# A planned attention and routing kernel: row maxima written twice, two partial sums kept in PSUM, the rests of units 0 and 1 moved to GpSimd, and the attention part written out in another order

## The chip, the cores and the metric

The kernel runs on one core of one Trainium2 chip. The metric is the time of one execution in microseconds of device time; lower is better. The engines are named as the profile names them: PE (TensorE), PEld (its weight loads), DVE (VectorE), ACT (ScalarE), POOL (GpSimd) and SP (SyncE, which here only issues DMA transfers; SPq is its queue).

## What is computed

Attention within clusters, followed by a greedy assignment of tokens to experts and an expert feed-forward layer. Cut to what matters:

```python
# q, k, v: (4, 8, 768, 64); centroids: (8, 16, 64)
q_assign = argmax(q_n @ c_n)          # cluster of each query, of each key
k_assign = argmax(k_n @ c_n)
scores = q @ k.T / 8, with -1e9 where q_assign != k_assign
scores = scores - max(scores, axis=-1)
attn = exp(scores) / (sum + 1e-9)
x = (attn @ v) as rows of 3072 tokens x 512
# experts: logits = x @ w_gate; tokens are handed out in order of
# falling logit, at most 384 per expert; then for each expert
out[mask] = relu(x[mask] @ w1[e]) @ w2[e]
```

## The kernel before

The kernel has two parts. The attention part works on eight units (a batch and four of its heads each); the part after it finds each expert's tokens, gathers their rows and runs the two matrix products. Every step of both parts is named in a long table of words, `ATT_ORDER` and `FFN_ORDER`; a loop calls the named functions one after the other, and that order is the order of the instructions on every engine. An engine takes its instructions strictly in that order; semaphores hold back an instruction whose inputs are not there.

**Splitting.** Each float32 input is scaled by 64 and split into two float16 halves, a high part and a rest: `split_hi` writes the high part on ACT (`L629`), `split_lo` the rest on DVE (`L633`, one instruction with both the loaded float32 tile and the high part as inputs). In unit 0 this is done head by head for q and k (128x384) and at once for v (128x1536); from unit 1 on each of q, k and v is one instruction of 128x1536. `load` fetches the inputs into four `ld` tiles that are used in turn, so that a load waits until the tile's former content has been split.

**Clusters and the two score products.** `cent` multiplies by the centroids, `hot0` to `hot5` (`hh` for unit 0) find the cluster of each row (`L667` to `L683`) and put a one-hot mark of +32768 or -32768 into extra columns of `qb` and `kb` (`L681`, `L683`). The four blocks qa, ka, qb, kb are transposed: by PE and copies in unit 0 (`pt`, `ptc`, `L720`, `L724` on ACT, `L726` on DVE), by DMA from unit 1 on (`trans`, `L714`). `m_mm` (`L761`) forms the scores in one layout, `m_rd` (`L765`, DVE) takes each row's maximum. `row0` and `row1` (`L775`, `L779`) turn twelve maxima into rows of a small tile `m2` (`qm` in unit 0), which `rowt` (`L783`) transposes by DMA and `row2` (`L787`) copies into rows 96 to 98 of `qbt`. `b_mm` (`L797`, `L801`) forms the scores again in the other layout, with the maxima subtracted by the matrix product, and `b_exp` (`L804`) takes the exponential on ACT. `res` (`L812`) forms the exponential's rest on POOL, and `av` (`L823` to `L829`) multiplies by v. So the second half of a unit's heads cannot begin `b_mm` before `rowt` and `row2` of that half have landed.

**Leaving a head.** `out0`, `out1`, `out2`, `hi0`, `hi1` (`L833` to `L852`) normalise a head and split it for the next product. `xtr` (`L861`) transposes two heads by DMA, `xst` (`L858`) stores them, and `lg0`, `lg1`, `lg2` (`L878`, `L885`, `L892`) add their share to the logits `L`. `lg1` sums a product from PSUM into `lt`; `lg2` adds `lt` to `L`. `vs`, `vact`, `vh2`, `vl2` (`L742` to `L752`) form a column mean of v: `vact` writes `vs`, `vh2` its high part `vmh`, `vl2` combines the two.

**Buffers that set who waits.** The score tiles `sc` have three PSUM buffers, released by `m_rd`, by `b_exp` or by a copy. The tile `mx` has one: `cent`, `vs` and `lg0` use it in turn. The accumulator `av` of a head has one, released by `hi1`. `wd` (`L652`) is a matrix product whose result nobody reads; it fills waits of PE at the start.

**The SP queue.** All loads, DMA transposes and the small transfers of the maxima stand in one queue on SP, each waiting in its place for what it needs.

Of the kernel before, what the change touches and what calls it, by code (L numbers as in the profile page):

```python
# [26 lines left out]
wd hh3,0 wd wd hh4,0,k dup,0,k,1 wd wd hh4,0,q split_lo,0,v,-,D hh5,0,k cent0,1,k hh5,0,q pt,0,kb,0 split_hi,0,q,3
pt,0,qb,0 cent0,1,q ptc,0,kb,0,A wd wd ptc,0,qb,0,D wd load,2,k,- wd split_hi,0,k,3 wd hh0,1 m_mm,0,0 dup,0,q,2 m_mm,0,1
hh1,1 m_mm,0,2 dup,0,k,2 hh2,1 wd hh3,1 wd dup,0,q,3 wd wd hh4,1,k wd hh4,1,q wd hh5,1,k split_lo,0,q,2,D vs,0 hh5,1,q
dup,0,k,3 split_lo,0,k,2,D split_lo,0,q,3,D wd wd split_lo,0,k,3,D vact,0 load,1,v,- wd wd vh2,0 wd wgs load,1,q,- wd wd  # L30
wd vl2,0 wd wd m_rd,0,0 wd wd wd wd wd m_rd,0,1 pt,0,kb,1 wd wd ptc,0,kb,1,A wd m_rd,0,2 pt,0,qb,1 wd wd ptc,0,qb,1,A wd
# [5 lines left out]
wd wd wd wd m_rd,0,3 wd wd wd wd wd m_rd,0,4 pt,0,qb,2 wd wd ptc,0,qb,2,A wd tab,9 pt,0,kb,3 tab,10 trans,1,qa,- tab,11
pt,0,qb,3 tab,12 ptc,0,kb,3,A tab,13 m_mm,0,5 ptc,0,qb,3,D wd wd dup,1,k,- m_rd,0,5 m_mm,0,6 m_mm,0,7 wd row0,0,0
m_mm,0,8 row1,0,0 m_rd,0,6 cent,1,k,0 dup,1,q,- cent,1,k,1 cent,1,k,2 m_rd,0,7 pt,0,qm,0 load,2,q,- cent,1,k,3
load,2,v,- ptc,0,qm,0,A wd m_rd,0,8 m_mm,0,9 wd split_hi,2,k,- wd wd m_rd,0,9 m_mm,0,10 m_mm,0,11 wd m_rd,0,10 m_mm,0,12  # L40
wd wd wd hot0,1,k b_mm,0,0 m_rd,0,11 wd wd b_exp,0,0 wd wd hot1,1,k m_mm,0,13 res,0,0,P wd row0,0,1 wd row1,0,1 wd
hot2,1,k wd wd m_rd,0,12 split_hi,2,q,- av,0,0 hot3,1,k pt,0,qm,1 b_mm,0,1 hot4,1,k ptc,0,qm,1,A m_rd,0,13 cent,1,q,0
hot5,1,k cent,1,q,1 cent,1,q,2 b_exp,0,1 trans,1,kb,- split_lo,2,k,-,D m_mm,0,14 cent,1,q,3 split_hi,2,v,- m_mm,0,15
b_mm,0,2 m_rd,0,14 res,0,1,P b_exp,0,2 hot0,1,q m_mm,0,16 res,0,2,P av,0,1 hot1,1,q trans,2,ka,- m_rd,0,15 av,0,2
hot2,1,q m_mm,0,17 m_rd,0,16 b_mm,0,3 dup,2,k,- hot3,1,q m_mm,0,18 hot4,1,q m_rd,0,17 load,3,q,- hot5,1,q b_exp,0,3
trans,1,qb,- row0,0,2 b_mm,0,4 row1,0,2 m_rd,0,18 res,0,3,P pt,0,qm,2 b_exp,0,4 tab,14 m_mm,0,19 tab,15 tab,16
ptc,0,qm,2,A m_mm,0,20 m_rd,0,19 res,0,4,P av,0,3 split_hi,3,k,- b_mm,0,5 m_rd,0,20 m_mm,0,21 av,0,4 m_rd,0,21 b_exp,0,5
b_mm,0,6 split_lo,2,q,-,D m_mm,0,22 b_exp,0,6 m_mm,0,23 cent,2,k,0 dup,2,q,- b_mm,0,7 m_rd,0,22 res,0,5,P cent,2,k,1
trans,2,qa,- cent,2,k,2 cent,2,k,3 b_exp,0,7 m_rd,0,23 m_mm,1,0 res,0,6,P av,0,5 row0,0,3 b_mm,0,8 row1,0,3 m_rd,1,0
pt,0,qm,3 res,0,7,P b_exp,0,8 out0,0,0 m_mm,1,1 out1,0,0 out2,0,0 ptc,0,qm,3,A b_mm,0,9 load,3,v,- m_rd,1,1 res,0,8,P  # L50
hi0,0,0 m_mm,1,2 b_exp,0,9 hi1,0,0 b_mm,0,10 m_rd,1,2 av,0,6 res,0,9,P b_exp,0,10 m_mm,1,3 tab,17 av,0,7 tab,18
split_hi,3,q,- m_rd,1,3 res,0,10,P b_mm,0,11 tab,19 tab,20 m_mm,1,4 tab,21 b_exp,0,11 hot0,2,k av,0,8 tab,22 m_rd,1,4
b_mm,0,12 tab,23 res,0,11,P m_mm,1,5 b_exp,0,12 tab,24 av,0,9 m_rd,1,5 b_mm,0,13 res,0,12,P tab,25 m_mm,1,6 b_exp,0,13
tab,26 av,0,10 m_rd,1,6 b_mm,0,14 res,0,13,P m_mm,1,7 tab,27 b_exp,0,14 av,0,11 tab,28 m_rd,1,7 b_mm,0,15 res,0,14,P
m_mm,1,8 out0,0,1 b_exp,0,15 out1,0,1 b_mm,0,16 out2,0,1 hi0,0,1 vl2,1 m_mm,1,9 split_lo,2,v,-,D b_exp,0,16 hi1,0,1
res,0,15,P load,4,k,- tab,29 xtr,0,0 av,0,12 m_rd,1,8 av,0,13 tab,30 m_rd,1,9 tab,31 b_mm,0,17 xst,0,0 res,0,16,P
m_mm,1,10 hot1,2,k b_exp,0,17 av,0,14 m_rd,1,10 b_mm,0,18 tab,32 res,0,17,P m_mm,1,11 tab,33 b_exp,0,18 av,0,15 tab,34
m_rd,1,11 b_mm,0,19 tab,35 tab,36 m_mm,1,12 row0,1,0 tab,37 b_exp,0,19 row1,1,0 av,0,16 res,0,18,P rowt,1,0 m_rd,1,12
b_mm,0,20 hot2,2,k m_mm,1,13 b_exp,0,20 av,0,17 res,0,19,P m_rd,1,13 b_mm,0,21 out0,0,2 m_mm,1,14 out1,0,2 b_exp,0,21
b_mm,0,22 res,0,20,P out2,0,2 row2,1,0 m_rd,1,14 hi0,0,2 m_mm,1,15 b_exp,0,22 res,0,21,P hi1,0,2 b_mm,0,23 m_rd,1,15  # L60
av,0,18 b_exp,0,23 av,0,19 res,0,22,P hot3,2,k m_mm,1,16 hot4,2,k av,0,20 m_rd,1,16 hot5,2,k res,0,23,P lg0,0,0 b_mm,1,0
trans,2,kb,- lg1,0,0 m_mm,1,17 b_exp,1,0 av,0,21 m_rd,1,17 b_mm,1,1 res,1,0,P cent,2,q,0 b_exp,1,1 cent,2,q,1 cent,2,q,2
cent,2,q,3 split_lo,3,k,-,D m_mm,1,18 av,0,22 b_mm,1,2 m_mm,1,19 hot0,2,q res,1,1,P trans,3,ka,- b_exp,1,2 av,0,23
hot1,2,q split_hi,3,v,- hot2,2,q res,1,2,P m_rd,1,18 dup,3,k,- hot3,2,q b_mm,1,3 hot4,2,q m_mm,1,20 load,4,q,- m_rd,1,19
hot5,2,q vs,2 b_exp,1,3 trans,2,qb,- out0,0,3 out1,0,3 out2,0,3 b_mm,1,4 res,1,3,P vact,2 m_rd,1,20 hi0,0,3 m_mm,1,21
b_exp,1,4 hi1,0,3 b_mm,1,5 vh2,2 m_rd,1,21 res,1,4,P av,1,0 b_exp,1,5 av,1,1 xtr,0,1 split_hi,4,k,- m_mm,1,22
# [1372 lines left out]
```

## Time and profile before

| what | value |
|---|---|
| median of 3 runs | 739.81 us |
| lowest and highest | 739.64 and 742.39 us |
| the profiled execution | 742.15 us |
| its span (first to last instruction) | 740.4 us |
| mean granted TensorE clock | 0.964 |
| first exponential of unit 0 | 46.0 us after the span's start |
| end of the attention part | about 437 us |

The profiled execution is 2.3 us above the median and 1.8 us above its own span. Busy time is a share of the span; a group's row gives line, engine, operation, output and inputs, count, total busy us and mean ns, and after the bar the idle time of the engine just before the group with what ended it. A row of the timeline gives start, duration and, in brackets, the idle time before it and its releaser. All positions are in us from the span's start.

### The profile page before, as it was taken

The numbers are of one execution on the slowest core, as the hardware profiler recorded it, in microseconds if no ns is written. First come the engines' busy times: TensorE is split into PE (matmuls) and PEld (weight loads), VectorE is DVE, ScalarE is ACT, GpSimd is POOL, SyncE is SP. The second block draws the span as 40 slices with busy tenths as digits, with TensorE's granted clock in tenths as the row PEclk, the third lists the DMA queues.
The fourth block names the chain that finished last, engine by engine and source line by source line (L and its number), as shares of the span: only waits on it lengthen the run. The fifth ranks groups of instructions, "written<-read, shape, count | busy, mean of one in ns | idle before, by whom it ended". The sixth has DMA issues, their size and how long they took to land. (4 is left out here: it accounts for less than half of the span.)

```text
span 740.4 us, 19763 instructions
## 1 busy us (share of the span) xinstructions
PE 669.7 (90%) x8274; PEld 444.9 (60%) x8274; DVE 545.1 (74%) x1170; ACT 420.9 (57%) x547; POOL 479.9 (65%) x369
## 2 busy tenths in 40 slices
...
GB/s 184 173 194 211 40 93 209 149 122 225 90 135 170 139 164 78 117 117 89 90 47 47 34 34 89 184 253 63 326 158 213 259 112 313 104 342 267 29 15 42
DMA packets 175451, 105.85 MB, mean 143 GB/s; under 512 B 135426, under 2 KB 160002, under 8 KB 175362
## 3 DMA queue, kind: packets, MB, share of 16 engines
...
## 5 line engine op out<-in xcount | busy, mean ns | idle before, releaser
L812 POOL TENSOR_TENSOR rt<-pt 128x768 f16<-128x768 f32 x181 | 281.4, 1571 | 139.3 <-ACT pt L804 136.4
L804 ACT ACTIVATE pt<-sc 128x768 f32<-128x768 f32 x192 | 154.6, 811 | 135.3 <-PE sc L801 120.6
L765 DVE TENSOR_REDUCE mxs<-sc 128x1 f32<-128x768 f32 x192 | 180.9, 951 | 39.5 <-PE sc L761 37.1
L823 PE MATMUL av<-vh,pt 128*128 128x66 f16 x1152 | 128.0, 196 | 9.8 <-DVE xb L852 9.8
L826 PE MATMUL av<-vh,rt 128*128 128x66 f16 x1152 | 127.7, 195 | 1.8 <-POOL rt L812 1.8
L1361 PE MATMUL pf<-xgt,w1h 128*128 128x384 f16 (+1 forms) x640 | 128.8, 293 | 0.3 <-DVE xgt L726 0.3
L825 PE MATMUL av<-vl,pt 128*128 128x64 f16 x1152 | 127.7, 194 | 0.0
L825 PEld LDWEIGHTS <-pt 128*128 128x128 bf16 x1152 | 108.1, 100 | 17.6 <-issue 8.7
L823 PEld LDWEIGHTS <-pt 128*128 128x128 bf16 x1152 | 108.8, 99 | 13.5 <-DVE xb L852 3.6
L797 PE MATMUL sc<-qbt,kbt 99*128 99x384 f16 x384 | 96.8, 334 | 17.8 <-DVE mxs L765 8.3
L826 PEld LDWEIGHTS <-rt 128*128 128x128 f16 x1152 | 107.6, 98 | 2.2 <-POOL rt L812 2.1
L761 PE MATMUL sc<-kbt,qbt 80*128 80x384 f16 x384 | 94.0, 329 | 10.2 <-DMA qbt<-qb 5.5
L801 PE MATMUL sc<-qat,kat 128*128 128x384 f16 x384 | 95.8, 331 | 0.0
L1361 PE MATMUL pf<-xgt,w1l 128*128 128x384 f16 (+1 forms) x320 | 89.9, 293 | 0.0
L1323 ACT ACTIVATE wr<-wr 128x1024 f32<-128x1024 f32 x64 | 66.7, 1046 | 24.9 <-PE pc L1279 23.2
L1361 PEld LDWEIGHTS <-w1h 128*128 128x128 f16 x640 | 57.3, 97 | 28.7 <-issue 1.1
L1399 PE MATMUL pf<-w2h,hh 128*128 128x512 f16 x192 | 72.6, 378 | 0.0
L1399 PE MATMUL pf<-w2l,hh 128*128 128x512 f16 x192 | 72.5, 378 | 0.0
L1399 PE MATMUL pf<-w2h,hl 128*128 128x512 f16 x192 | 72.5, 378 | 0.0
L1333 POOL TENSOR_TENSOR w2l<-wr,w2h 128x1024 f16<-128x1024 f32 x32 | 67.7, 2136 | 1.8 <-ACT w2h L1326 1.5
L1333 POOL TENSOR_TENSOR w1l<-wr,w1h 128x1024 f16<-128x1024 f32 x32 | 67.6, 2139 | 0.2
L1337 POOL DMA_INDIRECT xg<-xrow,idx x24 | 23.3, 972 | 60.6 <-DVE idx L1296 22.4
...
## 6 DMA issues: line engine op xcount, KB each, us to landing
...
xg<-xrow,idx POOLq DMA_INDIRECT x24, 6.3
```

Source lines behind the costliest of these rows:

```text
L761: nc.tensor.matmul(p[:, half, :S // 2], QBT[u][:D + C, i, :], KBT[u][:D + C, h * J + half * 3:h * J + half * 3 + 3, :], start=True, stop=True)
L765: nc.vector.tensor_reduce(mxs[u % 3][:, i:i + 1], MP.pop((u, i))[:, :, :S // 2], axis=AX.XY, op=OP.max)
L797: nc.tensor.matmul(ps[:, half, :S // 2], KBT[u][:ER + 3, s, :], QBT[u][:ER + 3, cs, :], start=True, stop=False)
L801: nc.tensor.matmul(ps[:, half, :S // 2], KAT[u][:, s, :], QAT[u][:, cs, :], start=False, stop=True)
L804: nc.scalar.activation(pts[(u * 12 + s // 2) % RP][:, s % 2], MP.pop((u, "b", s))[:, :, :S // 2], AF.Exp, scale=ESC)
L812: (nc.vector if e == "D" else nc.gpsimd).tensor_sub(rts[x][:, s % 2], p.rearrange("p a b -> p (a b)"), hi_view(pts[x])[:, s % 2])
L823: nc.tensor.matmul(o[:, j, :], hi[:, js], VH[u][:, s, :], start=(kt == 0 and j == 0), stop=False, skip_group_check=True)
L825: nc.tensor.matmul(o[:, j, :D], hi[:, js], VL[u][:, s, :], start=False, stop=False, skip_group_check=True)
L826: nc.tensor.matmul(o[:, j, :], r[:, js], VH[u][:, s, :], start=False, stop=(kt == J - 1), skip_group_check=True)
L1333: nc.gpsimd.tensor_sub(lo, wrs[c], hi)
L1361: nc.tensor.matmul(o, (w1l if i == 2 else w1h)[x][:, c, fs], xgt[x][:, h + int(i == 1), ts], start=(first and i == 0), stop=(last and i == ...
L1399: nc.tensor.matmul(PS["o", p, g], (hl if i == 2 else hh)[x][:, f, g * P:(g + 1) * P], (w2l if i == 1 else w2h)[x][:, f, :], start=(f == 0 ...
```

## The change

There are five edits.

1. `row0` writes the maxima twice, into columns 98 and 99 of the small tile (`qm`) or two blocks of it (`m2`), through an input view in which every maximum is repeated; `row1` already had that input view. `row2` copies the same three rows as before.
2. `lt` and `vs` no longer are tiles in SBUF: they are further columns of the PSUM tile `mx` that their sources stand in. So `mx` now is held until `lg2` and `vl2`.
3. In units 0 and 1, `split_sc` scales the loaded tile in place on ACT, `split_hi` copies it without a scale, and `split_lo` is a subtraction on POOL. Units 2 to 7 keep the old form (`D`).
4. Fifteen `memset`s of the routing tables go from DVE to POOL.
5. `ATT_ORDER` is another order of the same steps: 91 instead of 109 `wd`, more of unit 0's copies on DVE (`ptc` with `D`), and other places for the transfers (in unit 4, `rowt` of the second half stands ahead of `load,7,v` instead of behind it). `out2` gets an argument for its engine; it is `D` everywhere, as before. `FFN_ORDER` is unchanged.

```diff
+    def split_sc(u, name, hh):
+        src, hi, lo = parts(u, name, hh)
+        nc.scalar.activation(src, src, AF.Copy, scale=SQ)
-    def split_hi(u, name, hh):
+    def split_hi(u, name, hh, e):
         src, hi, lo = parts(u, name, hh)
-        nc.scalar.activation(hi, src, AF.Copy, scale=SQ)
+        nc.scalar.activation(hi, src, AF.Copy, scale=SQ if e == "D" else 1.0)
     def split_lo(u, name, hh, e):
         src, hi, lo = parts(u, name, hh)
-        (nc.vector if e == "D" else nc.gpsimd).scalar_tensor_tensor(lo, src, SQ, hi, op0=OP.mult, op1=OP.subtract)
+        if e == "D":
+            nc.vector.scalar_tensor_tensor(lo, src, SQ, hi, op0=OP.mult, op1=OP.subtract)
+        else:
+            nc.gpsimd.tensor_sub(lo, src, hi)
...
     def vsum(u):
-        PC["v"] = pmx.tile([P, HG, D], F32, name="mx")
+        w = pmx.tile([P, 2, HG, D], F32, name="mx")
+        PC["v"], PC["vs"] = w[:, 0], w[:, 1]
...
-        nc.vector.scalar_tensor_tensor(vms[u % 3][ee, :, :D], vmh_[ee], rest[ee], vs[ee], op0=OP.mult, op1=OP.add)
+        nc.vector.scalar_tensor_tensor(vms[u % 3][ee, :, :D], vmh_[ee], rest[ee], PC["vs"][ee], op0=OP.mult, op1=OP.add)
...
+    def twice(u, cs):
+        return mxs[u % 3][:, cs, None].to_broadcast([P, cs.stop - cs.start, 2])
     def row0(u, g):
         e, m, cs = rows(u, g)
-        nc.vector.tensor_scalar(m, mxs[u % 3][:, cs], -(2.0 ** 29), -1.0 / BIG, op0=OP.max, op1=OP.mult)
+        nc.vector.tensor_scalar(m, twice(u, cs), -(2.0 ** 29), -1.0 / BIG, op0=OP.max, op1=OP.mult)
...
-        PC["l"] = p = pmx.tile([P, J, 2, E], F32, name="mx")
+        w = pmx.tile([P, 3, J, E], F32, name="mx")
+        PC["lt"] = w[:, 2]
...
-            nc.vector.scalar_tensor_tensor(lb, lt, 0.0, lb, op0=OP.add, op1=OP.add)
+            nc.vector.scalar_tensor_tensor(lb, PC["lt"], 0.0, lb, op0=OP.add, op1=OP.add)
...
-            vec(nc.vector.memset, o, float(1 << sh))
+            fill(o, float(1 << sh))
```

Of the table, the same place in unit 5, before and after (`b_mm` and `b_exp` now stand one step nearer to the `av` that uses them):

```diff
-m_rd,6,2 hi0,5,0 res,5,8,P row2,5,1 m_mm,6,3 b_exp,5,10 cent,7,k,3 hi1,5,0 b_mm,5,11 m_rd,6,3 res,5,9,P av,5,6
+row2,5,1 cent,7,k,3 b_exp,5,9 res,5,8,P hi1,5,0 b_mm,5,10 m_rd,6,3 av,5,6 b_exp,5,10 res,5,9,P av,5,7 hot0,7,k m_mm,6,4
```

What stands in a row on the engines at the places that matter below. First ACT at the start, before: high parts (`qa`, `ka`, `vh` from `ld`), copies of a high part (`qb`, `kb`), transposed blocks leaving PSUM (`L724`) and marks from `ceq`.

```order
L629 ACTIVATE qa<-ld_76 128x6x64
L629 ACTIVATE ka<-ld_75 128x6x64
L638 ACTIVATE qb<-qa 128x6x64
L629 ACTIVATE qa<-ld_76 128x6x64
L629 ACTIVATE ka<-ld_75 128x6x64
L640 ACTIVATE kb<-ka 128x6x64
L629 ACTIVATE qa<-ld_76 128x6x64
L724 ACTIVATE qat_112<-sc 128x768
L629 ACTIVATE vh_106<-ld_77 128x24x64
L629 ACTIVATE ka<-ld_75 128x6x64
L724 ACTIVATE kat_115<-sc 128x768
```

Each 128x384 or 128x1536 tile is one pass here, and its high part is copied soon after.

The same place on ACT after the change, with the scaling in place (`L630`) as instructions of their own:

```order
L630 ACTIVATE ld_76<-ld_76 128x384
L630 ACTIVATE ld_75<-ld_75 128x384
L634 ACTIVATE qa<-ld_76 128x6x64
L634 ACTIVATE ka<-ld_75 128x6x64
L630 ACTIVATE ld_76<-ld_76 128x384
L630 ACTIVATE ld_75<-ld_75 128x384
L634 ACTIVATE qa<-ld_76 128x6x64
L634 ACTIVATE ka<-ld_75 128x6x64
L630 ACTIVATE ld_77<-ld_77 128x1536
L634 ACTIVATE vh_106<-ld_77 128x24x64
L646 ACTIVATE qb<-qa 128x6x64
L648 ACTIVATE kb<-ka 128x6x64
```

Two passes stand where one stood, and the copies of the high part of head 0 moved behind v.

DVE at the start, before, from the rest of head 0's q to the first cluster maximum (`cmx`):

```order
L633 SCALAR_TENSOR_TENSOR qa<-ld_76,qa 128x6x64
L547 COPY ct<-mx 128x256
L633 SCALAR_TENSOR_TENSOR ka<-ld_75,ka 128x6x64
L633 SCALAR_TENSOR_TENSOR qa<-ld_76,qa 128x6x64
L726 COPY kat_115<-sc 128x768
L633 SCALAR_TENSOR_TENSOR ka<-ld_75,ka 128x6x64
L726 COPY qat_112<-sc 128x768
L667 TENSOR_REDUCE cmx<-mx 128x12
```

The four rests of heads 0 and 1 (`L633`) and two of the copies are DVE's.

DVE at the same place after the change, from the first copy of a transposed block:

```order
L734 COPY qat_112<-sc 128x768
L526 CAST cst<-sq 128x64
L734 COPY kat_115<-sc 128x768
L526 TENSOR_TENSOR cst<-sq,cst 128x64
L734 COPY qat_112<-sc 128x768
L526 TENSOR_TENSOR cst<-sq,cst 128x64
L552 TENSOR_SCALAR wg<-wgf 128x4x8
L553 SCALAR_TENSOR_TENSOR wg<-wgf,wg 128x4x8
L549 COPY ct<-mx 128x256
L734 COPY kat_115<-sc 128x768
L675 TENSOR_REDUCE cmx<-mx 128x12
```

The rests are gone from it; all four copies of the first two heads are DVE's, and the table of centroids (`cst`, `ct`) is made between them.

SP before, around the transposes of unit 3's `qb` (into `qbt_118`) and unit 4's `ka` and `qa`:

```order
L714 DMA_TRANSPOSE kat_116<-ka 128x24x128
L714 DMA_TRANSPOSE qat_113<-qa 128x24x128
L486 DMA ld_75<-in_q_dram 128x4x384
L486 DMA ld_76<-in_v_dram 128x4x384
L714 DMA_TRANSPOSE qbt_118<-qb 128x24x128
L861 DMA_TRANSPOSE xt_150<-xb_146 128x12x128
L858 DMA xrow<-xb_146 768x1x256
L486 DMA ld_77<-in_k_dram 128x4x384
L783 DMA_TRANSPOSE mt_145<-m_94 128x1x128
L787 DMA qbt_120<-mt_145 3x12x128
```

The transpose of `qb` waits for both transposes of unit 4 and two loads.

SP at the same place after the change:

```order
L722 DMA_TRANSPOSE kat_116<-ka 128x24x128
L488 DMA ld_75<-in_q_dram 128x4x384
L722 DMA_TRANSPOSE qbt_118<-qb 128x24x128
L877 DMA_TRANSPOSE xt_149<-xb_145 128x12x128
L874 DMA xrow<-xb_145 768x1x256
L722 DMA_TRANSPOSE qat_113<-qa 128x24x128
L795 DMA_TRANSPOSE mt_144<-m_94 128x1x128
L488 DMA ld_76<-in_v_dram 128x4x384
L488 DMA ld_77<-in_k_dram 128x4x384
L799 DMA qbt_120<-mt_144 3x12x128
```

The transpose of `qb` now stands ahead of that of `qa` and of the load of v, and these two stand ahead of the last steps of unit 2's maxima instead.

More of the change, by code (lines that the diff above doesn't have):

```diff
@@ L27 @@
[L27 to L31, printed above, removed]
@@ L37 @@
[L37 to L41, printed above, removed]
@@ L42 @@
[L42 to L66, printed above, removed]
@@ L67 @@
-split_lo,3,q,-,D av,1,2 b_mm,1,6 xst,0,1 m_mm,1,23 b_exp,1,6 m_rd,1,22 res,1,5,P av,1,3 trans,3,qa,- av,1,4 dup,3,q,-
-m_rd,1,23 b_mm,1,7 res,1,6,P m_mm,2,0 row0,1,1 b_mm,1,8 row1,1,1 b_exp,1,7 m_rd,2,0 av,1,5 b_exp,1,8 res,1,7,P m_mm,2,1
-out0,1,0 b_mm,1,9 m_rd,2,1 rowt,1,1 m_mm,2,2 b_exp,1,9 res,1,8,P lg0,0,1 out1,1,0 b_mm,1,10 out2,1,0 load,4,v,- m_rd,2,2
-m_mm,2,3 hi0,1,0 res,1,9,P b_exp,1,10 hi1,1,0 b_mm,1,11 row2,1,1 split_hi,4,q,- lg1,0,1 av,1,6 lg2,0,1 m_rd,2,3
-res,1,10,P av,1,7 b_exp,1,11 m_mm,2,4 av,1,8 m_rd,2,4 res,1,11,P m_mm,2,5 av,1,9 m_rd,2,5 b_mm,1,12 b_mm,1,13 vl2,2
@@ L122 @@
-res,4,4,P m_rd,4,22 av,4,2 b_mm,4,6 dup,6,q,- vl2,5 m_mm,4,23 split_lo,6,v,-,D av,4,3 xtr,3,1 b_mm,4,7 b_exp,4,6 av,4,4
-b_exp,4,7 m_rd,4,23 res,4,5,P m_mm,5,0 xst,3,1 cent,6,k,0 cent,6,k,1 load,7,v,- row0,4,1 b_mm,4,8 row1,4,1
-split_hi,7,q,- m_rd,5,0 rowt,4,1 res,4,6,P m_mm,5,1 av,4,5 m_rd,5,1 b_mm,4,9 b_exp,4,8 res,4,7,P cent,6,k,2 out0,4,0
-out1,4,0 b_exp,4,9 m_mm,5,2 out2,4,0 b_mm,4,10 m_rd,5,2 hi0,4,0 res,4,8,P row2,4,1 m_mm,5,3 b_exp,4,10 cent,6,k,3
-hi1,4,0 b_mm,4,11 m_rd,5,3 res,4,9,P av,4,6 b_exp,4,11 av,4,7 hot0,6,k m_mm,5,4 hot1,6,k res,4,10,P av,4,8 m_rd,5,4
```

306 lines of the change are left out of this document (179 added, 127 removed).

## The prediction

> **What bounds the kernel now.** I read the page first, then the busy times by stretch, then the waits, then the groups of DVE, and last the time line of the SP queue at the longest wait.
>
> ```profile
> PE 669.7 (90%) x8274; PEld 444.9 (60%) x8274; DVE 545.1 (74%) x1170; ACT 420.9 (57%) x547; POOL 479.9 (65%) x369
> ```
>
> ```profile
> core 0: us, PE busy (x) PEld busy (x) DVE busy (x) ACT busy (x) POOL busy (x), PEclk, DMA share, GB/s
> 0.00:46.00 46.00, 36.92 (x404) 25.95 (x405) 39.59 (x92) 31.01 (x50) 7.02 (x28) 1.00 0.68 186
> 46.00:107.00 61.00, 49.02 (x692) 34.33 (x691) 52.66 (x86) 32.90 (x40) 39.44 (x31) 0.92 0.56 122
> 107.00:339.00 232.00, 206.60 (x3493) 154.19 (x3491) 204.02 (x293) 138.05 (x176) 178.68 (x113) 0.98 0.72 142
> 339.00:432.00 93.00, 86.91 (x1471) 65.13 (x1468) 76.38 (x118) 47.23 (x67) 64.63 (x45) 0.98 0.31 56
> 432.00:740.00 308.00, 290.29 (x2231) 165.31 (x2227) 172.45 (x582) 171.66 (x217) 190.15 (x153) 0.95 0.52 168
> ```
>
> Over the whole span PE is the busiest, but the change leaves the last stretch (the expert part, PE 290.3 of 308) alone, so I cost that at nothing, with PE as its cover. In the first 339 us PE and DVE are both busy for close to nine tenths. Who waits for whom from 107 to 339, PE first, then DVE:
>
> ```profile
> PE sc L797 <- DMA qbt<-mt: 8.2, 3, 3.8
> PE sc L761 <- DMA qbt<-qb: 5.5, 2, 4.3
> ```
>
> ```profile
> DVE mxs L765 <- PE sc L761: 23.3, 22, 4.9
> ```
>
> DVE's 28 idle us (232 less 204) are nearly all a wait for PE's scores, and PE's longest waits are for two DMA transfers. So the stretch is a row of dense DVE work, broken by a few DMA waits that stop PE and then DVE. Shortening DVE's work shortens the dense pieces; it doesn't shorten a piece whose length a DMA chain sets.
>
> **The short DVE operations.** The same stretch, by group:
>
> ```profile
> L775 DVE TENSOR_SCALAR m<-mxs 128x12 f16<-128x12 f32 x9 | 7.0, 776 | 0.3
> L892 DVE SCALAR_TENSOR_TENSOR L<-lt,L 128x48 f32<-128x48 f32 x7 | 6.2, 888 | 0.2
> L752 DVE SCALAR_TENSOR_TENSOR vm<-vmh,rest,vs 2x256 f16<-2x256 f16 x5 | 4.7, 948 | 0.2
> L779 DVE TENSOR_SCALAR m<-mxs 128x24 f16<-128x24 f32 x9 | 1.9, 216 | 0.0
> L885 DVE TENSOR_REDUCE lt<-mx 128x48 f32<-128x96 f32 x7 | 1.7, 248 | 0.0
> ```
>
> Twelve columns take 776 ns, while twenty-four take 216 ns in the next instruction, from the same maxima, through the repeated view. `row0` gets exactly that view, so I price it at 216: 9 x (776 - 216) = 5.0 us. `lg2` gets one PSUM input; its neighbour `L885`, with a PSUM input alone, takes 248 for twice the elements read, so 7 x (888 - 248) = 4.5 us. For `vl2` the time line has one that ran while POOL was idle:
>
> ```profile
> 21.26 0.49 DVE L752 SCALAR_TENSOR_TENSOR vm<-vmh,rest,vs 2x256 f16<-2x256 f16 x1 [0.34 <-ACT vmh L749]
> ```
>
> At 0.49 it gives 5 x (948 - 490) = 2.3 us. Together 11.8 us; the other end is nothing, if the long durations belong to the operation and not to its operands. What they are not is the comparison as against the arithmetic, since a comparison on a contiguous SBUF tile is long as well:
>
> ```profile
> L917 DVE TENSOR_SCALAR sel<-sel 128x128 f16<-128x128 f16 x2 | 2.2, 1080 | 0.0
> ```
>
> Here the Trainium skill speaks against one part. Its page "Vector Engine (DVE) Microarchitecture Reference" (section 5.1, Performance modes) says that a one-source operation whose input is read with a step of 0 still ran in the mode that uses both ports, and "SBUF — State Buffer" (Who interferes with whom) that such an operation blocks against GpSimd. By them `row0` would stay at 776, and 5.0 of the 11.8 us would be missing; `row1`'s 216 ns in the same view, with POOL busy 178.7 of 232 us around it, says otherwise, and I go by that row.
>
> Not all 11.8 us reach the end. Three pieces of this stretch are timed by a chain on the SP queue, from the transpose of `qb` to the landing of the second half's maxima. In unit 1 that chain runs from here
>
> ```profile
> 115.25 5.37 SPq L714 DMA_TRANSPOSE qbt<-qb  x1
> 135.53 0.50 PE L797 MATMUL sc<-qbt,kbt 99*128 99x384 f16 x2 [2.44 <-DMA qbt<-mt]
> ```
>
> to PE's restart, 20 us. With two more like it, 60 of 232 us, or 26%, are such that a faster DVE only lengthens the wait: 8.7 us are left. PE is at 206.6 of 232 itself, which leaves it 25.4 to give; the last unit before 339 has little of that, so I take 7. Operations of these kinds before 107 and after 339 I cost at nothing, the cover being the start's own chain and PE's 86.9 of 93.
>
> **The transfers.** The longest wait, with SP ahead of it:
>
> ```profile
> 162.32 4.23 SPq L714 DMA_TRANSPOSE qat<-qa  x1
> 167.24 0.50 SPq L486 DMA_DIRECT2D ld<-in_v_dram  x1
> 168.26 6.36 SPq L714 DMA_TRANSPOSE qbt<-qb  x1
> 177.99 0.52 PE L761 MATMUL sc<-kbt,qbt 80*128 80x384 f16 x2 [4.33 <-DMA qbt<-qb]
> ```
>
> Unit 3's `qb` is transposed behind `qa` and the loads of q and v, and takes 6.36 us beside them. The change puts the `qa` transpose and the load of v behind it, so `qb` begins at least the load's 0.50 us earlier and loses less to loads. But `qa`'s 4.23 us and two loads now stand ahead of unit 2's `rowt` and `row2`, which PE waits for later. Ends: -4.3 (wait gone) and 0 (it comes back at `row2`); I take -3, nearer the first, because unit 2's second half has no such wait now. In unit 4, `rowt` now goes ahead of the load of v, where PE waited too:
>
> ```profile
> 284.34 0.82 PE L797 MATMUL sc<-qbt,kbt 99*128 99x384 f16 x2 [2.02 <-DMA qbt<-mt]
> 236.25 0.76 PE L797 MATMUL sc<-qbt,kbt 99*128 99x384 f16 x2 [3.75 <-DMA qbt<-mt]
> ```
>
> I take -1 for the first (-2.0 to +1.7, since `row2` still follows the load, as at 236, where the wait is 3.75). The wait at 236 and the one at 135.5 keep the same transfers ahead of them and stay.
>
> **The start.** DVE before 46 us, and ACT:
>
> ```profile
> L633 DVE SCALAR_TENSOR_TENSOR vl<-ld,vh 128x1536 f16<-128x1536 f32 x2 | 3.5, 1750 | 0.0
> L633 DVE SCALAR_TENSOR_TENSOR qa<-ld,qa 128x384 f16<-128x384 f32 x4 | 2.2, 551 | 0.0
> L633 DVE SCALAR_TENSOR_TENSOR ka<-ld,ka 128x384 f16<-128x384 f32 x4 | 2.2, 550 | 0.0
> L633 DVE SCALAR_TENSOR_TENSOR qa<-ld,qa 128x1536 f16<-128x1536 f32 x1 | 1.8, 1752 | 0.0
> L633 DVE SCALAR_TENSOR_TENSOR ka<-ld,ka 128x1536 f16<-128x1536 f32 x1 | 1.7, 1748 | 0.0
> L726 DVE COPY qbt<-sc 128x768 f16<-128x768 f16 x2 | 1.1, 558 | 0.4 <-PE sc L720 0.3
> L917 DVE MEMSET wdig<- 128x128 bf16 x7 | 1.2, 165 | 0.0
> ```
>
> ```profile
> L629 ACT ACTIVATE qa<-ld 128x384 f16<-128x384 f32 x4 | 2.1, 517 | 4.5 <-DMA ld<-in_q_dram 4.5
> L629 ACT ACTIVATE vh<-ld 128x1536 f16<-128x1536 f32 x2 | 3.0, 1478 | 0.0
> L724 ACT ACTIVATE kbt<-sc 128x768 f16<-128x768 f16 x3 | 2.4, 811 | 2.2 <-PE sc L720 2.1
> 9.09 0.52 ACT L629 ACTIVATE qa<-ld 128x384 f16<-128x384 f32 x1 [3.93 <-DMA ld<-in_q_dram]
> 12.34 0.36 DVE L667 TENSOR_REDUCE cmx<-mx 128x12 f32<-128x192 f32 x1
> 45.98 0.81 ACT L804 ACTIVATE pt<-sc 128x768 f32<-128x768 f32 x1
> L812 POOL TENSOR_TENSOR rt<-pt 128x768 f16<-128x768 f32 x181 | 281.4, 1571 | 139.3 <-ACT pt L804 136.4
> ```
>
> DVE loses the rests (11.4 us) and the fills (1.2) and gains five copies (5 x 0.56 = 2.8): -9.8. ACT gains eight scalings of 0.52 and three of 1.48 (8.6) and gives up five copies of 0.81 (4.0): 35.6 of 46 instead of 31.0. POOL, idle here but for 7 us, takes the rests; by its row for 768 elements I estimate 0.79 us for 384 and 3.14 for 1536, 15.7 in all.
>
> Does the first exponential come earlier? Head 1's q reaches ACT at 9.09 in either order. Two scalings and two high parts (2.1) end at 11.2; POOL's second rest ends near 12.2; then PE's transposes (0.8, as for the others), the centroids, a copy and the cluster product: the first cluster maximum comes at about 15.0, against 12.34. After that DVE has 39.6 - 9.8 + 2.2 = 32.0 us before the first exponential (the 2.2 are cluster steps of unit 1 that stood behind it), about 6.5 of them done by 15.0, and a gap of some 3 while head 0's marks go round ACT and PE: 43.7. A mark and ACT's table load follow, so 45.5 to 46.5: no earlier than 45.98, with 2.2 us less left for DVE. I take -1. Ends: -9.8, if nothing but DVE mattered, and +6.2, if ACT idles as often as before (15.0, less 3.9 for the load): 9.09 + (35.6 - 3.6) + 11.1 = 52.2.
>
> **What it may add.** `mx` is held until `lg2` or `vl2`, so PE's next `cent` may wait for one short DVE step; `b_mm` stands one step nearer to `av`; a new order makes new waits. I allow +2, between 0 and +5 (what PE now waits for `qb`'s transposes, 5.5, nearly once more).
>
> **Sum.** -1 - 7 - 3 - 1 + 2 = -10. The profiled execution took 742.15 (span 740.4) and would take 732.1; the median, 739.81, is 2.3 below it, and becomes 730.
>
> **Rivals.**
> - The start gains in full: -9.8 in place of -1 gives 721. For it, DVE's 39.6 of 46; against, ACT's filled queue.
> - The repeated view doesn't help (the two pages' rule, above): 5.0 us lost, 735. Against it, the 216 ns.
> - The DMA waits only move: the 4 us of both transfer terms are gone, 734. For it, 236.25, where loads stand ahead of `row2`, as they now do in unit 2.
> - Nothing changes: PE's own work is the floor, and DVE's shorter steps turn into idle time. PE's 206.6 of 232 speaks for it, its waits against; only 1 us is left of the sum, 739.
> - Slower: `av` waits for POOL's rest. `b_mm` is one step nearer, and POOL is busy 178.7 of 232 us, so a rest that ends late now stops PE. Before this was rare:
>
> ```profile
> PE av L826 <- POOL rt L812: 1.8, 3, 1.1
> ```
>
> One such wait of 0.6 (1.8 / 3) in each of 28 heads is 17 us: 747. It outweighs the gains from 0.36 us a head on.
>
> **How the numbers follow.** My forecast has 0.55, with a range of 724 to 736; the full start 0.10; the view 0.08; the moved waits 0.12; nothing 0.07; slower 0.08. From 721 to 740 all but the last and the edges of the first two lie inside. Half a per cent, 3.7 us, is about what can be told from no change: below 736.1 are the first four, less some of the last two of them: 0.77. Within it are the fifth and that edge, 0.14. Slower, with other new waits in the order, 0.09.
>
> **What would show it.** `row0` near 0.22 us, `lg2` near 0.25 and `vl2` near 0.5 each (one of them as before: that term is wrong). The first exponential at 45.5 to 46.5; at 40 the full start is right, past 52 ACT is the bound. No wait over 2 us for `qbt<-qb`, and those at 135 and 236 still there. PE's wait for POOL's rest under 5 us in all. I am wrong altogether if unit 1 to unit 4 take as long as before though DVE's short steps have shrunk.

## The result, and the profile after

| kernel | median of runs | ratio to the kernel before, 95% interval |
|---|---|---|
| before | 741.1 us (739.64 to 744.41, 4 runs) | |
| after | 709.45 us (707.4 to 713.07, 4 runs) | 0.9572 (0.9516 to 0.9629) |

The change takes 31.7 us off the median. 10 were forecast, to 730, with a range of 724 to 736 for the forecast itself and of 721 to 740 with most of the rivals; the measured time lies below both. The profiled execution of after took 707.99 us. Its busy times, over the span and by stretch (the stretches of the prediction, moved to the same events):

```profile
PE 659.0 (93%) x8256; PEld 438.0 (62%) x8256; DVE 525.8 (74%) x1149; ACT 425.2 (60%) x554; POOL 500.7 (71%) x395
```

```profile
0.00:46.00 46.00, 35.01 (x392) 23.86 (x393) 34.89 (x83) 34.95 (x55) 29.24 (x57) 1.00 0.69 195
46.00:101.00 55.00, 50.06 (x807) 36.30 (x804) 50.52 (x79) 35.33 (x44) 40.51 (x26) 1.00 0.76 147
101.00:320.00 219.00, 207.66 (x3518) 155.33 (x3517) 200.35 (x300) 139.96 (x179) 184.28 (x122) 0.98 0.76 150
320.00:405.00 85.00, 79.55 (x1398) 59.98 (x1394) 70.81 (x120) 44.56 (x63) 56.89 (x40) 0.99 0.27 55
405.00:706.00 301.00, 286.72 (x2157) 162.53 (x2157) 169.23 (x571) 170.39 (x215) 189.75 (x153) 0.95 0.53 170
```

In the third row PE does 207.7 us of work in 219; before it did 206.6 in 232. The work hardly changed, the idle time went from 25 to 11 us. The waits of that row, of PE and then of DVE:

```profile
PE sc L809 <- DVE mxs L774: 7.3, 14, 1.0
PE sc L770 <- DMA qbt<-qb: 2.0, 1, 2.0
```

```profile
DVE mxs L774 <- PE sc L770: 11.3, 15, 1.6
```

The 8.2 us for `qbt<-mt` (the transposed maxima) are gone in this execution, and DVE's wait for PE has halved (23.3 before). PE's longest wait is 2.0 us. The three short operations in the same stretch, with `row1` as the second row:

```profile
L788 DVE TENSOR_SCALAR m<-mxs 128x24 f16<-128x24 f32 x10 | 8.4, 840 | 0.3
L792 DVE TENSOR_SCALAR m<-mxs 128x24 f16<-128x24 f32 x10 | 2.2, 216 | 0.0
L761 DVE SCALAR_TENSOR_TENSOR vm<-vmh,rest,mx 2x256 f16<-2x256 f16 x5 | 2.4, 489 | 0.3 <-ACT vmh L758 0.2
L910 DVE SCALAR_TENSOR_TENSOR L<-mx,L 128x48 f32<-128x48 f32 x7 | 1.5, 207 | 0.2
```

`lg2` (`L910`) went from 888 to 207 ns and `vl2` (`L761`) from 948 to 489. `row0` (`L788`) did not get shorter: 840 ns, 776 before. The start's end, on ACT:

```profile
45.94 1.28 ACT L816 ACT_TABLE_LOAD   x1
47.23 0.81 ACT L816 ACTIVATE pt<-sc 128x768 f32<-128x768 f32 x1
```

From the first exponential of each unit the change of the span is laid out by place. All times are in us, from the time line of ACT:

| stretch | before | after | difference |
|---|---|---|---|
| start to the first exponential | 46.0 | 47.2 | +1.2 |
| unit 0 (to unit 1's first exponential) | 60.9 | 50.6 | -10.3 |
| units 1 to 4 | 200.9 | 182.9 | -18.0 |
| units 5 and 6 | 84.2 | 83.8 | -0.4 |
| unit 7, to its last exponential | 37.6 | 32.4 | -5.2 |
| the rest | 310.8 | 309.3 | -1.5 |
| span | 740.4 | 706.2 | -34.2 |

Here are the two stretches that carry it, unit 0 and units 1 to 4, by engine (PE, PEld, DVE, ACT, POOL, then the granted clock). First before, then after:

```profile
46.00:106.90 60.90, 48.92 (x691) 34.29 (x690) 52.66 (x86) 32.80 (x39) 39.44 (x31) 0.92 0.56 122
106.90:307.80 200.90, 176.60 (x2966) 131.31 (x2965) 174.01 (x249) 118.58 (x149) 151.61 (x96) 0.97 0.73 146
```

```profile
47.20:97.80 50.60, 45.66 (x715) 32.76 (x713) 46.30 (x71) 32.47 (x41) 38.26 (x24) 1.00 0.73 143
97.80:280.70 182.90, 173.01 (x2918) 129.16 (x2917) 168.53 (x252) 118.14 (x149) 152.38 (x101) 0.98 0.77 156
```

PE's idle time falls by 7.0 us in unit 0 (60.90 - 48.92 against 50.60 - 45.66) and by 14.4 in units 1 to 4. PE's busy time falls by 6.9 in both together, for nearly the same number of products (3657 and 3633). That second part is the clock: 0.92 of 60.9 us and 0.97 of 200.9 mean some 22 us at half the clock; 0.98 of 182.9 means 7. The 28.3 us of these two stretches are thus 21.4 of waits and 6.9 of clock.

### The profile page after: what moved, and what is told of

The parts are those of the page before. It is cut to its first block, busy times and chain, and to the rows that moved or that the text cites. A ratio compares the mean times of both kernels' runs of the same rounds, so it can differ in the third digit from the quotient of the medians.

```text
span 706.2 us, 19751 instructions
## 1 busy us (share of the span) xinstructions
PE 659.0 (93%) x8256; PEld 438.0 (62%) x8256; DVE 525.8 (74%) x1149; ACT 425.2 (60%) x554; POOL 500.7 (71%) x395
## 5 line engine op out<-in xcount | busy, mean ns | idle before, releaser
L835 PE MATMUL av<-vh,pt 128*128 128x66 f16 x1152 | 125.4, 195 | 2.3 <-DVE xb L868 1.9
L838 PE MATMUL av<-vh,rt 128*128 128x66 f16 x1152 | 125.0, 194 | 1.4 <-POOL rt L824 1.4
L837 PE MATMUL av<-vl,pt 128*128 128x64 f16 x1152 | 125.0, 192 | 0.0
L837 PEld LDWEIGHTS <-pt 128*128 128x128 bf16 x1152 | 106.6, 99 | 13.0 <-issue 4.0
L835 PEld LDWEIGHTS <-pt 128*128 128x128 bf16 x1152 | 107.4, 98 | 10.0 <-issue 0.3
L809 PE MATMUL sc<-qbt,kbt 99*128 99x384 f16 x384 | 94.8, 328 | 9.5 <-DVE mxs L774 8.9
L1344 ACT ACTIVATE wr<-wr 128x1024 f32<-128x1024 f32 x64 | 66.7, 1046 | 26.8 <-PE pc L1300 23.3
L1358 POOL DMA_INDIRECT xg<-xrow,idx x24 | 23.3, 969 | 60.0 <-DVE idx L1317 22.1
```

What stands on the lines that cost most here:

```text
L809: nc.tensor.matmul(ps[:, half, :S // 2], KBT[u][:ER + 3, s, :], QBT[u][:ER + 3, cs, :], start=True, stop=False)
L835: nc.tensor.matmul(o[:, j, :], hi[:, js], VH[u][:, s, :], start=(kt == 0 and j == 0), stop=False, skip_group_check=True)
L837: nc.tensor.matmul(o[:, j, :D], hi[:, js], VL[u][:, s, :], start=False, stop=False, skip_group_check=True)
L838: nc.tensor.matmul(o[:, j, :], r[:, js], VH[u][:, s, :], start=False, stop=(kt == J - 1), skip_group_check=True)
```

## The experiments

Theory 1: the new order of the table carries the gain, since the second pass (`b_mm`, `b_exp`, `res`) stands later against the maxima and other work is spread better. Theory 2: the gain comes from the lighter DVE, as the prediction had it. Unit lengths of the kernels tested, in us from the profiled executions:

| kernel | median, ratio | first exp. | unit 0 | 1 to 4 | 5 and 6 | unit 7 |
|---|---|---|---|---|---|---|
| new order alone | 716.97, 0.9648 | 50.2 | 52.2 | 184.0 | 84.8 | 33.7 |
| PSUM alone | 734.35, 0.9883 | 45.9 | 60.8 | 196.8 | 82.9 | 34.6 |
| GpSimd alone | 749.17, 1.0084 | 54.4 | 59.4 | 201.7 | 83.9 | 37.6 |
| old order, pass later | 739.47, 0.9968 | 52.1 | 56.0 | 198.7 | 83.1 | 37.8 |
| after, pass earlier | 713.3, 0.9627 | 46.1 | 48.0 | 191.3 | 83.7 | 33.4 |
| after, pass later | 739.96, 0.9972 | 49.6 | 58.8 | 196.6 | 88.5 | 32.9 |
| new order to unit 1 | 734.34, 0.991 | 50.5 | 52.3 | 196.4 | 83.9 | 37.7 |
| new order from unit 1 | 725.59, 0.979 | 46.1 | 62.4 | 187.0 | 84.8 | 33.2 |
| new order to unit 4 | 720.8, 0.9726 | 50.3 | 52.3 | 182.6 | 84.0 | 37.7 |
| after, sums in SBUF | 715.49, 0.9653 | 47.8 | 52.2 | 184.4 | 84.9 | 35.2 |

**The parts by themselves.** The new order with all the old operations:

```diff
 ATT_ORDER = the new table, without split_sc, all split_lo on DVE
-        nc.vector.tensor_scalar(m, twice(u, cs), -(2.0 ** 29), -1.0 / BIG, op0=OP.max, op1=OP.mult)
+        nc.vector.tensor_scalar(m, mxs[u % 3][:, cs], -(2.0 ** 29), -1.0 / BIG, op0=OP.max, op1=OP.mult)
+    vs, lt = tiles in SBUF again; the fills on DVE again
```

> The new order of the attention with the old operations: sums of logits and values in SBUF, the rests of units 0 and 1 and the fills on DVE, the row of maxima in plain form. Theory 1 (the order carries the gain: the step of the exponentials stands one place later against the maxima, so PE no longer waits for their transposition, and less of PE's time runs at the half clock): 713 to 720 us, no wait of PE for QBT<-mt over 1 us in units 1 to 4. Theory 2 (the short operations and the rests on GpSimd carry it, as the prediction's sum had it): 731 to 738 us. If the new order needs the lighter start to be worth anything: 725 to 731 us.

716.97 us, 0.9648 (0.9619 to 0.9676): 25.4 of the 31.7 us, so the order carries the gain, as theory 1 says. DVE does all its old work here, and units 1 to 4 still need only 184.0 us. The stretch by engine, and PE's waits in it for the two transfers:

```profile
102.40:286.40 184.00, 171.52 (x2918) 128.55 (x2917) 173.90 (x252) 118.20 (x149) 152.18 (x101) 0.99 0.75 155
```

```profile
PE sc L773 <- DMA qbt<-qb: 1.4, 1, 1.4
PE sc L813 <- DMA qbt<-mt: 0.7, 2, 0.4
```

Before they were 5.5 and 8.2 us. So 11.6 of the 16.9 us by which units 1 to 4 get shorter are these waits, and some 4 are the half clock (0.97 of 200.9 us before, 0.99 of 184.0 here). DVE is as busy as before (173.9 and 174.0 us).

Now the old order with the two PSUM sums (those of the values from unit 3 on):

```diff
-            nc.vector.scalar_tensor_tensor(lb, lt, 0.0, lb, op0=OP.add, op1=OP.add)
+            nc.vector.scalar_tensor_tensor(lb, PC["lt"], 0.0, lb, op0=OP.add, op1=OP.add)
+        PC["v"], PC["vs"] = w[:, 0], (w[:, 1] if u > 2 else vs)
```

> The old order and operations, with the logit sums in PSUM and the value sums in PSUM for units 3 to 7 (for units 0 to 2 they stay in SBUF, since the old order puts the operation that frees the bank far behind). Theory 1: 736 to 740 us; lg2 0.21 us, and the 1.5 us of it near 408 us that hold the last unit's output are gone. Theory 2 (the prediction's sum: 4.5 + 1.5 us of DVE less a quarter): 734 to 737 us.

734.35 us, 0.9883 (0.985 to 0.9915), 8.0 us: theory 2's range for this part, and 3.0 of it in unit 7, where the prediction had set nothing.

The old order with the rests of units 0 and 1 on GpSimd:

```diff
-split_hi,0,q,0 ... split_lo,0,q,0,D
+split_sc,0,q,0 split_hi,0,q,0,P ... split_lo,0,q,0,P
-        vec(nc.vector.memset, t, x)
+        steps.append(("POOL", lambda: nc.gpsimd.memset(t, x)))
```

> The old order with the rests of units 0 and 1 and the table fills on GpSimd, and the scaling by ScalarE ahead of them. Theory 1: 738 to 745 us, no gain, since the old order reads the rests as early as before. Theory 2 (DVE's 8 us of rests were what held unit 0 up): 728 to 735 us, with unit 0 some 8 us shorter.

749.17 us, 1.0084 (1.0058 to 1.011): 6.9 us slower. The first exponential comes at 54.4. DVE is busy 24.3 us of the first 46 instead of 39.6, but it stands still: in the old order its copies of the transposed blocks come up while PE's transposes, which wait for the rests, are late (the longest such wait before was 0.4 us).

```profile
0.00:46.00 46.00, 32.79 (x324) 22.87 (x325) 24.30 (x65) 34.70 (x57) 27.18 (x46) 1.00 0.52 154
```

```profile
DVE qbt L739 <- PE sc L733: 9.3, 2, 4.8
```

**The place of the second pass.** In the kernel before, the second pass of units 0 to 6 one place later:

```diff
-m_mm,4,3 b_exp,3,10 hi1,3,0 row2,3,1 b_mm,3,11 split_hi,6,q,- m_rd,4,3 res,3,9,P av,3,6
+m_mm,4,3 b_exp,3,9 hi1,3,0 row2,3,1 b_mm,3,10 split_hi,6,q,- m_rd,4,3 res,3,8,P av,3,6
```

> The kernel before, in which only the products of the second pass, their exponentials and their rests of units 0 to 6 stand one place later against everything else (and six attention operations that would read what is not there yet go behind them). Theory 1 (the lead of the maxima's transposition decides): PE's waits for QBT<-mt fall from 8.2 us to under 2 us in units 1 to 4, and the time to 727 to 734 us. Theory 2 (the waits only move): 738 to 745 us.

755.6 us, 1.0169 (1.0143 to 1.0196). The waits for the maxima did fall, and another took their place:

```profile
PE sc L803 <- DMA kat<-ka: 16.2, 4, 5.7
...
PE sc L799 <- DMA qbt<-mt: 1.7, 2, 1.4
```

I had moved `b_mm` of step 23 past the transposition that refills its ring buffer, so in units 1 to 4 that step used a later unit's keys and waited for them. This run says nothing of theory 1's time; the next is the same with that mended:

```diff
-res,1,22,P trans,4,ka,- dup,4,k,- cent,3,q,1 b_mm,1,23 m_rd,2,17
+res,1,22,P dup,4,k,- cent,3,q,1 b_mm,1,23 trans,4,ka,- m_rd,2,17
```

> The second pass of units 0 to 6 one place later in the kernel before, as in the run before it, and now with the transpositions of the first key block of units 4 to 7 placed behind the last product that reads the same ring buffer (in the run before it they stood ahead, so that the last step of four units read the keys of a later unit, and PE waited 16 us for their transfer). Theory 1 (the lead of the maxima decides): waits for QBT<-mt under 2 us, none for KAT, 727 to 735 us. Theory 2 (the old order has no room for a later second pass; the waits come back as waits for the rests, for the output block and for banks): 740 to 750 us.

739.47 us, 0.9968 (0.9948 to 0.9988). Theory 1's range is missed by 4.5 us, theory 2's by half a microsecond. The maxima no longer stop PE, but by the table the start is 6.1 us longer, and units 1 to 4 gain only 2.2 us, at a granted clock of 0.97 as before. In the old order the later second pass alone is worth 2 us. And `av` now stands so close behind `res` that it waits for GpSimd (1.8 us before):

```profile
PE av L828 <- POOL rt L814: 6.6, 9, 1.3
```

The opposite edit in the kernel after:

```diff
-m_mm,4,3 b_exp,3,9 res,3,8,P hi1,3,0 b_mm,3,10 m_rd,4,3 av,3,6
+m_mm,4,3 b_exp,3,10 res,3,9,P hi1,3,0 b_mm,3,11 m_rd,4,3 av,3,6
```

> The kernel after, in which only the products of the second pass, their exponentials and rests of units 0 to 6 stand one place earlier, which is where the kernel before had them. Theory 1 (the lead decides): waits for QBT<-mt come back, 6 to 12 us in units 1 to 4, and the time is 716 to 724 us. Theory 2 (the place of the second pass is worth nothing): 706 to 711 us.

713.3 us, 0.9627 (0.9604 to 0.965), against 0.9572 and 0.9591 for after in its two comparisons: 3 to 4 us slower by the medians, with intervals that overlap, and between the two ranges. The profile is clearer: the waits come back nearly as theory 1 says, and units 1 to 4 take 8.4 us longer; that the start and unit 0 would take 3.7 less, neither theory had:

```profile
PE sc L811 <- DMA qbt<-mt: 5.6, 4, 3.6
```

**Where in the order.** Two tables were joined: one up to a certain product, and behind it what is left, in the sequence of the other (old operations throughout).

```diff
 ATT_ORDER = new table up to b_mm,1,0; then the old table without the steps already done
```

> Old operations throughout. The new order up to the first product of unit 1's second pass, and behind it the old order of what is left. Theory 1 (the two stretches add up): unit 1's first exponential at 102.4 us as with the new order alone (106.9 before), the rest as before: 735 to 739 us. Rival (all of the gain is in the first unit, where the work is put that holds up the rest): 717 to 725 us.

```diff
 ATT_ORDER = old table up to b_mm,1,0; then the new table without the steps already done
```

> Old operations throughout. The old order up to the first product of unit 1's second pass, and behind it the new order of what is left. Theory 1 (the two stretches add up): unit 1's first exponential at 106.9 us, and the rest as with the new order alone: 719 to 724 us. Rival (all of the gain is in the first unit): 735 to 742 us.

734.34 us, 0.991 (0.9875 to 0.9945), and 725.59 us, 0.979 (0.9767 to 0.9813). Losses to before of 6.9 and 15.6 us add up to 22.5 of the 25.4: the stretches nearly add, and the larger part lies behind unit 0. The first is 0.7 us under the theory's range, the second 1.6 above. By the profile of the first, 4.1 us are gained up to unit 1's first exponential, and another 4.5 in units 1 to 4, although the old order rules there.

**Undoing parts of after.**

```diff
-        PC["v"], PC["vs"] = w[:, 0], w[:, 1]
+        PC["vs"] = vs
-        PC["lt"] = w[:, 2]
+        PC["lt"] = lt
```

> The kernel after, with the logit sums and value sums back in SBUF. Theory 1 (in the new order DVE is 92% busy in units 1 to 4, so its short operations count nearly in full): 6 to 9 us slower than after, 715 to 719 us. Rival (the order has hidden them: with the new order alone units 1 to 4 already took 184.0 us against 182.9 after): 1 to 4 us slower, 710 to 714 us.

715.49 us, 0.9653 (0.9627 to 0.9679): by the ratios 4.6 to 6.0 us slower than after, theory 1's range of times. Its reason does not hold: in units 1 to 4, where DVE is busy 168.5 of 182.9 us after and 172.7 here, these 4.2 us cost 1.5. By the profiles 1.6 more are lost in unit 0, 1.1 in units 5 and 6, and 2.8 in unit 7, where PE waits 2.6 us for the output block `xb` and not 1.6. A short operation does not count nearly in full.

```diff
-split_sc,0,q,0 split_hi,0,q,0,P ... split_lo,0,q,0,P
+split_hi,0,q,0,D ... split_lo,0,q,0,D
```

> The kernel after, with the rests of units 0 and 1 and the table fills back on DVE. Theory 1 (the rests on GpSimd are worth what the start shows: first exponential at 50.2 us with the new order alone, 47.2 after): 712 to 715 us. Rival (GpSimd's rests gain nothing, as with the old order, where they cost 7 us): 706 to 710 us.

710.66 us, 0.959 (0.9562 to 0.9617), between the two expectations and not to be told from after's 0.9572 and 0.9591. The first exponential is at 51.0, 3.8 us later than after's, and 1.5 of that is regained by the end of unit 7 (399.2 against 396.9). What the rests and fills on GpSimd gain is 0 to 1.3 us by the ratios and 2.3 by the profiles, and not clear of noise.

The two operations of the row of maxima, the other way round:

```diff
-row0,3,0 av,2,16 row1,3,0 b_exp,2,18
+row1,3,0 av,2,16 row0,3,0 b_exp,2,18
```

> The kernel after, with row1 ahead of row0; both are in the repeated form. Theory 1 (the first of the two waits for the end of GpSimd's operation and pays for both, whatever its form): row1 then takes 0.8 to 1.0 us in the mean and row0, behind it, 0.2 us; time 707 to 711 us. Theory 2 (the operation of row0, a maximum and a product, is the slow one): row0 stays at 0.8 to 1.0 us and row1 at 0.22 us.

708.22 us. Now `row1` (`L795`) takes 917 ns in the mean and `row0` (`L791`) 214. The same place in unit 4, after and swapped, with the operation that GpSimd has under way (two rests, the second ending at 227.33 and 226.75):

```profile
222.93 4.40 POOL L824 TENSOR_TENSOR rt<-pt 128x768 f16<-128x768 f32 x2
225.36 0.94 DVE L774 TENSOR_REDUCE mxs<-sc 128x1 f32<-128x768 f32 x1
226.34 1.07 DVE L788 TENSOR_SCALAR m<-mxs 128x24 f16<-128x24 f32 x1
227.27 0.22 DVE L792 TENSOR_SCALAR m<-mxs 128x24 f16<-128x24 f32 x1
```

```profile
222.36 4.39 POOL L827 TENSOR_TENSOR rt<-pt 128x768 f16<-128x768 f32 x2
225.77 1.07 DVE L795 TENSOR_SCALAR m<-mxs 128x24 f16<-128x24 f32 x1
226.71 0.21 DVE L791 TENSOR_SCALAR m<-mxs 128x24 f16<-128x24 f32 x1
```

Whichever comes first lasts until 0.08 us past the end of GpSimd's operation. So it is in all 14 cases of `row0` in units 1 to 7 after: its end follows the end of one of GpSimd's by 0.08 or 0.09 us. Theory 1. In the kernel before the plain `row0` did the same in its 14 cases, 0.03 us behind, so the repeated view had nothing to shorten.

The traces also show why the second is short. Of the 224 second operations in the 16 profiles that have the pair on DVE, 221 took under 0.3 us, and none of these began after GpSimd's next operation. The other three (in before, with PSUM alone and with GpSimd alone) began 0.06 to 0.09 us after it, and lasted until 0.08 or 0.09 us past its end. In before, where a copy of 0.18 us stands between the two operations:

```profile
97.40 1.49 POOL L812 TENSOR_TENSOR rt<-pt 128x768 f16<-128x768 f32 x1
```

```profile
97.49 1.49 DVE L779 TENSOR_SCALAR m<-mxs 128x24 f16<-128x24 f32 x1
```

**What bounds it now.** After again, beside the next three on one chip:

> The kernel after, unchanged, on the same chip as the three runs beside it, so that they can be compared with it: 0.953 to 0.961 of before, 707 to 711 us.

711.14 us, 0.9591 (0.9565 to 0.9618). In this second profile PE waits 3.2 us for `qbt<-mt` with the span at 706.5, so these waits are wholly gone in the first profile only. The longest, 2.75 us, is in unit 2, the one unit of 1 to 4 in which `row2` of the second half stands behind the same product (step 10) as before. The two operations of the row on GpSimd:

```diff
-        nc.vector.tensor_scalar(m, twice(u, cs), ...
-        nc.vector.tensor_scalar(e, twice(u, cs), ...
+        nc.gpsimd.tensor_scalar(m, twice(u, cs), ...
+        nc.gpsimd.tensor_scalar(e, twice(u, cs), ...
```

> The kernel after, with the two operations of the row of maxima (row0 0.91 us and row1 0.22 us, 14 of each and 4 smaller of each in the first unit) on GpSimd. Theory 1 (DVE bounds units 1 to 4): 16 us of DVE go, DVE waits for PE more and PE less, 700 to 706 us. Theory 2 (PE bounds, since its waits for DVE are 6 us in units 1 to 4): 705 to 709 us. Rival: the rows wait behind a rest on GpSimd (1.6 us each), the lead of the transposition shrinks and PE waits for QBT<-mt again: 710 to 716 us.

707.54 us, 0.9537 (0.9511 to 0.9563), the lowest median of all: 3.6 us under after beside it. The intervals miss each other by 0.0002, after's first comparison (0.9516 to 0.9629) takes this one in, and the profiles show no gain (spans 707.3 and 706.5), so whether there is one stays open. DVE is relieved in units 1 to 4, and their time stays, 184.0 us against 182.9. The first 182.9 of them (DVE 168.53 in after's):

```profile
97.80:280.70 182.90, 172.13 (x2908) 127.94 (x2906) 161.01 (x236) 116.97 (x149) 153.50 (x117) 0.98 0.75 155
```

Less DVE work does not shorten the stretch here: theory 2. The second pass of after one place later still, with the same care for the ring buffers:

```diff
-m_mm,4,3 b_exp,3,9 res,3,8,P hi1,3,0 b_mm,3,10 m_rd,4,3 av,3,6
+m_mm,4,3 b_exp,3,8 res,3,7,P hi1,3,0 b_mm,3,9 m_rd,4,3 av,3,6
```

> The kernel after, with the second pass of units 0 to 6 one place later still (and the transpositions of the first key block of units 4 to 7 behind the last reader of their buffer). Theory 1 (the lead of 9 us that the new order gives is enough, so more buys nothing, and the first unit starts a step later): 709 to 716 us. Theory 2 (more lead takes away the waits that are left): 700 to 706 us.

739.96 us, 0.9972 (0.9951 to 0.9993). Both theories are far off: 29 us are lost to a wait that none of them had priced.

```profile
PE av L841 <- POOL rt L827: 26.1, 36, 1.8
```

In this row of the table the last rest ahead of `av,3,6` is that of step 9 before, of step 8 after, and of step 7 here. After stands at the last place at which GpSimd keeps up.

```diff
 ATT_ORDER = new table up to b_mm,4,0; then the old table without the steps already done
```

> Old operations throughout. The new order up to the first product of unit 4's second pass, and behind it the old order of what is left. Theory (the stretches add up): unit 4's first exponential at 240 us as with the new order alone (259.9 before), then the old pace: 721 to 725 us. Rival (the gain sits in unit 4 and the last): 728 to 735 us.

720.8 us, 0.9726 (0.9691 to 0.9762), as the stretches say. With the run to unit 1 this puts some 14 us down to the rows from unit 1's second pass to unit 4's (by the profiles 10.8 in units 1 to 3 and 3.0 in unit 4), and some 4 to unit 7 (37.7 here, 33.7 with the new order throughout).

Last, another share of DVE's work, moved to ScalarE (with the rows on GpSimd):

```diff
-out2,3,1,D
+out2,3,1,A
```

> The kernel after, with the rows of maxima on GpSimd, and the division of the outputs of heads 1 and 3 of units 0 to 6 (one operation of 0.57 us on DVE each, 14 in all) as six activations each on ScalarE. Theory 1 (DVE still counts): another 8 us of DVE go, 700 to 705 us. Theory 2 (PE and the order bound; DVE's load no longer counts): 706 to 710 us. Rival (ScalarE's six operations stand ahead of an exponential and hold up the second pass): 711 to 720 us.

724.64 us, 0.9765 (0.9736 to 0.9793): the rival's direction, 4.6 us beyond its range. Six activations of 287 ns take the place of one DVE operation of 566, and `av` waits for its bank meanwhile:

```profile
L857 ACT ACTIVATE av<-av,rc 128x64 f32<-128x64 f32 x54 | 15.5, 287 | 1.6
```

```profile
PE av L838 <- DVE xb L871: 17.2, 11, 2.4
```

## Why the prediction was wrong, step by step

- **The order: the step that failed.** The prediction priced the new table at -3 and -1 for two transfers and +2 for new waits, -2 in all. By itself it measures -25.4. I read the order at the four DMA waits over 2 us and let the rest stand. What went, by the profile of the new order alone: 16.9 us in units 1 to 4 (11.6 of waits for the two transfers, some 4 of half clock), 4.5 in the start and unit 0 together, 3.9 in unit 7. Of the four waits' 12.5 us the prediction had counted 4.
- **"The cover being the start's own chain and PE's 86.9 of 93".** With this, work before 107 and after 339 was costed at nothing. Unit 0 alone lost 10.3 us and unit 7 5.2. PE's waits for the output block `xb` (before, from 46 to 107 and from 390 to 440; then after, from 363 to 406) could be moved; PE's busy share said nothing on that:

```profile
PE av L823 <- DVE xb L852: 3.2, 1, 3.2
...
PE av L823 <- DVE xb L852: 4.3, 3, 1.7
```

```profile
PE av L835 <- DVE xb L868: 1.6, 1, 1.6
```

- **"The wait at 236 and the one at 135.5 keep the same transfers ahead of them and stay."** They went. The transfers ahead were as I said, but `b_mm`, which waits, had moved one place back against `row2`. I had counted that shift only as a risk (the slower rival: `av` waits for GpSimd's rest). It was both: undoing it brings 5.6 us of waits for the maxima back (after itself had none and 3.2 in its two profiles), and one place more costs 26.1 us of waits for rests. After itself waits 1.4 us for rests, as forecast (under 5).
- **`row0` at 216 ns.** Wrong: 840 in the stretch, 909 over all 14. I took the repeated view for the reason that `row1` is short, but `row1` was short because it began ahead of GpSimd's next operation. The stretch that I read left out the one of 14 in before that took 1.49 us; its mean over the span is 307 ns, not 216. The rival of the view was mis-sized as well: cut by the sum's own share, 7 of 11.8, its 5.0 us are 3.0, and it comes to 733. The Trainium skill's pages "Vector Engine (DVE) Microarchitecture Reference" (section 5.1, Performance modes) and "SBUF — State Buffer" (Who interferes with whom) had it right for the first of the two: a step of 0 doesn't keep such an operation from blocking against GpSimd.
- **`lg2` and `vl2`.** The durations were right: 207 and 489 ns against 248 and 490 forecast. The worth, 6.8 us less a quarter, 5.1, against 4.6 to 6.0 measured by undoing them in after, was right by luck: it was meant for the stretch from 107 to 339, and units 1 to 4 gave 1.5; more came from units 0 and 7, which were costed at nothing. On the old order they were worth 8.0, 4.1 of them in units 1 to 4. The sign that units 1 to 4 get shorter could not tell, since the order alone shortens them to 184.0.
- **The start.** -1 was near enough in sum (0 to 2.3 us by undoing it), but the first exponential came at 47.2 and not at 45.5 to 46.5, so the sign was not seen: the new order alone puts it at 50.2, and the rests on GpSimd bring 3.0 of that back. On the old order the same edit costs 6.9.
- **The clock.** The sum took a wait at its length. The trace of before shows PE at half the clock behind the three longest of them in units 0 to 4, for example behind the 3.21 us that end at 89.6 and the 3.75 that end at 236.25 (the last three numbers are the clock, the DMA share and GB/s):

```profile
89.60:93.00 3.40, 3.36 (x46) 2.85 (x46) 2.47 (x4) 0.00 (x0) 1.04 (x2) 0.50 0.72 194
...
236.30:239.70 3.40, 3.40 (x27) 2.10 (x27) 1.38 (x2) 0.81 (x1) 1.07 (x1) 0.51 0.01 3
```

Of the 28.3 us in units 0 to 4, 6.9 are this and were in no term.

What stays open: which single moves within the new order take the waits away. With the second pass where it stood, units 1 to 4 of after still take 191.3 us against 200.9, and PE waits 8.2 us for the two transfers against 13.7; the PSUM sums explain 1.5 to 4.1 of the rest. For the start, unit 0 and unit 7 no run moves single steps. Whether the rows on GpSimd gain 3.6 us is open too, since the profiles don't show them.
